# A transformer block on one core: the first expert item is chosen from twelve token tiles, and its first four product blocks stand between the last attention units

## The chip, the cores and the metric

The kernel runs on one core of a Trainium2 chip. The metric is the device time of one execution in microseconds (us). A core has five engines with queues of their own: TensorE (PE, with its weight loads PEld), VectorE (DVE), ScalarE (ACT), GpSimd (POOL) and the DMA queues, here nearly all issued from SyncE (SP). Each engine takes its instructions in the order in which they were recorded and waits on semaphores of the others.

## The reference

```python
# 1. windowed attention, 4 batches x 8 heads x 576 positions x 64
scores = where(0 <= i - j < 128, q @ k.T / 8 - slope[h] * |i - j|, -1e9)
x = softmax(scores) @ v                      # then [2304, 512], heads side by side
# 2. mixture of experts, one of 8 experts for each token
logits = x @ w_gate + modality_bias[modality_id]
e = argmax(logits);  gate = softmax(logits)[e]
x = gate * (relu(x @ w1[e]) @ w2[e])         # w1 512x1024, w2 1024x512
# 3. dense block
h = x @ w_in;  out = (h * cos(h)) @ w_out    # 512x2048, 2048x512
```

## The kernel before

Every fp32 product is made as three products of rounded parts (high by high, high by low, low by high), so each operand that comes from memory is split first: ScalarE casts the high part, VectorE subtracts it to get the low part. A split of a piece of weights (128 by 1024) is one CAST `s<-r` on ACT and one TENSOR_TENSOR `s<-r,s` on DVE.

**Attention.** There are 36 units: 18 tiles of 128 tokens, each in two halves of four heads. For a unit, `score(n)` makes the products q by k on PE, the masked minimum on DVE (`sx`) and the exponentials on ACT (`e`); `flip(n)` transposes the exponentials on PE, copies them on ACT (`pT`, `pa`) and masks them on POOL; `pv(n)` multiplies by v on PE and divides on DVE (`den`, then `xt` or `y`) into a tile X. The one accumulator bank O that `pv` writes must have been read by that division before the next `pv` may start. When both halves of a tile are there, it is stored to x_dram, and `xt_split` transposes it and splits it into xT.

**Routing.** For each pair of tiles, `logits(t)` gives three calls: the products with the gate weights (PE `bk<-xT,wg`, ACT `ls`), `choose` (two transposes of `ls` on PE, then eight short operations on DVE that end in `ohb`), and `ranks` (eight products of `ohb` and `cum` on PE, then DVE). `early()` picks the expert with most tokens so far, computes the row numbers of 256 of its tokens, gathers them from x_dram (an indirect DMA from POOL into xg, two halves) and loads that expert's first weights: this is item 0. In this kernel it looks at sixteen tiles (TE = T - 2). `late()` makes the full plan once all 18 tiles are ranked: `sums`, `slots` (ends in `oa<-oa,row` on DVE), `table` (18 products `oa` by `ob` on PE, then the row numbers `idx`), and `behind_slots` (ends in `regs<-ie`, the expert of each item, which SP reads before it can load that expert's weights).

**Items.** Nine items of 256 tokens follow. An item has eight up blocks (`up`: 12 products `xT,s` of 128x256) and eight down blocks (12 products `hh,s`), the downs three blocks behind the ups. `to_xT` transposes the two gathered halves and splits them (ACT CAST and DVE TENSOR_TENSOR `xT`).

**What sets the order.** In attention up to the fourth unit from the end PE and POOL are held to the written order; after that, the loop still calls score, flip and pv, and the calls in the list `after` (the logits of the last four tiles, `early()`, ...) are dealt out between them, while a list scheduler is free to order PE. In the items from block 12 to 67 the order is held again. Item 0's weights are split, and its rows transposed, only after the attention's pools are closed (the `split_w1(0, 0)`, `to_xT(0, 0)` lines ahead of the item loop).

Of the kernel before, what the change touches and what calls it, by code (L numbers as in the profile page):

```python
# [29 lines left out]
def kernel(  # L30
# [25 lines left out]
    UNITS = NE - 1  # L56
    NBLK = 2 * MIN_ITEMS + UNITS
    NL = MIN_ITEMS + UNITS
    TE = T - 2
# [160 lines left out]

    E = {}
# [41 lines left out]
    def early():  # L263
        eo = rt.tile([128, NE], F32, name="eo")
        w0 = rt.tile([128, TE], F32, name="w0")
        oa0 = rt.tile([128, TE, 2], F16, name="oa0")

        def first():
            m = rt.tile([128, 2], F32, name="em")
# [5 lines left out]
            V_.tensor_scalar(eo, rev, m[:, 1:2], None, op0=ALU.is_equal)  # L275
            fold(w0, oh[:, 0:TE], eo.unsqueeze(1).to_broadcast([128, TE, NE]), [128, TE, NE], rt)
            V_.tensor_tensor(w0, w0, row[:, 0:TE], op=ALU.mult)
            one_hot(oa0, 2, pf[:, 0, 0:TE], TE)
# [20 lines left out]
        return [first, second, order]  # L299
# [3 lines left out]
    def late():  # L303
# [116 lines left out]
        def rows_of():  # L420
# [4 lines left out]
            V_.tensor_tensor(dt, dt, rank, op=ALU.add)  # L425
            di = rt.tile([128, T], I32, name="di")
# [35 lines left out]
    def gather(i, u=None):  # L462
        for j in range(2 if u is None else 1):
# [13 lines left out]


# [23 lines left out]
    with ExitStack() as c:  # L502
# [261 lines left out]
        def pv(n):  # L764
# [11 lines left out]
            if hg == 0:  # L776
                X[t] = gp.tile([128, DM], F32, name="y") if t >= TE else xp.tile([128, DM], F32, name="xt")
# [3 lines left out]
            if hg == 1:  # L781
                with ExitStack() as w:
                    if t >= TE:
# [3 lines left out]
                if t < TE - 2:  # L787
                    later(p, 0, lambda: xt_split(t))
                else:
                    after.append(lambda: xt_split(t))  # L790
                if t % 2:
                    calls = logits(t - 1)
                    if t < TE - 2:
                        later(p, 1, calls[0])
                        later(p + 1, 0, calls[1])
                        later(p + 2, 1, calls[2])
                    else:
                        after.extend(calls)
                if t == TE - 1:
                    after.extend(early())  # L800

        def xt_split(t):
# [3 lines left out]
            for kk in range(KD):  # L806
                nc.tensor.transpose(pt[:, kk], X[t][:, 128 * kk:128 * kk + 128], ident)
            nc.scalar.copy(xT[:, 0, :, c0:c0 + 128], pt)
            nc.vector.tensor_tensor(xT[:, 1, :, c0:c0 + 128], pt, xT[:, 0, :, c0:c0 + 128].bitcast(F32),
                                    op=ALU.subtract)  # L810
# [49 lines left out]
        after, due = [], {}  # L860
# [55 lines left out]
        for n in range(N + 2):  # L916
# [4 lines left out]
            nc.tensor.on = n <= END + 1  # L921
# [5 lines left out]
            if n > END:  # L927
                calls([after.pop(0) for _ in after[:2]])
# [15 lines left out]
            if n > END:  # L944
                calls([after.pop(0) for _ in after[:2 if n < N + 1 else 1]])
        assert not due

    nc = tc.nc
    banks(S=2, T=2, P=2, O=1)
# [6 lines left out]
    W1, W2, HH, ACC = {}, {}, {}, {}  # L956
    NF = FF // 128
# [29 lines left out]
    def load_y(g, j, yT):  # L987
        yT = YT[g] = yT.rearrange("p a (k c) -> p a k c", k=KD)[:, :, :, 0:128 * groups[g][1]]
# [119 lines left out]
    with ExitStack() as c:  # L1108
# [3 lines left out]
        def split_w1(i, g):  # L1112
            s1 = W1[i, g] = s1s[(NF // 2 * i + g) % len(s1s)]
            r1 = R1.pop((i, g))
            nc.scalar.copy(s1[:, 0], r1)
            nc.vector.tensor_tensor(s1[:, 1], r1, s1[:, 0].bitcast(F32), op=ALU.subtract)

# [8 lines left out]
        def up(i, f):  # L1126
            g, j = divmod(f, 2)
            w, xT = W1[i, g], xTs[i % 2]
            if j == 0:
                HH[i, g] = bank("S", [128, 2, SLOTS])  # L1130
            ph = HH[i, g]
            for kk in range(KD):
                for a, b in ((0, 0), (0, 1), (1, 0)):
                    nc.tensor.matmul(ph[:, j], w[:, a, kk, 128 * j:128 * j + 128], xT[:, b, kk],
                                     start=kk == 0 and a == 0 and b == 0, stop=kk == KD - 1 and a == 1)
# [68 lines left out]
        split_w1(0, 0)  # L1204
        to_xT(0, 0)
        after.pop(0)()
        xt = to_xT(0, 1)
        after.pop(0)()
        split_w1(0, 1)
        after.pop(0)()  # L1210
        with tc.issue_after(xt[0].ins), tc.issue_after(MK["oh"].ins):
            splits(2, 1)
        for n in range(len(steps) + LAG):
# [67 lines left out]
            with ExitStack() as later:  # L1281
# [3 lines left out]
                if n < len(steps) and not InOrder.on:  # L1285
                    splits((n + 1) // 2 + 3, n // 2 + 1)
# [195 lines left out]
```

## Time and profile before

| | |
|---|---|
| median of 3 runs | 840.37 us (837.58 to 842.68) |
| profiled execution | 839.8 us, of which the span from first to last instruction is 838.1 us |
| busy share of the span | PE 95%, PEld 84%, DVE 73%, ACT 59%, POOL 24% |
| mean granted TensorE clock | 0.988 of full speed |

The span divides into attention with routing (0 to about 180 us), the expert items (about 180 to 420 us) and the dense block. The change touches the seam between the first two, about 153 to 226 us. A share of busy time says little there, since PE is nearly always busy on both sides of it; the rows of the seam itself are needed.

### The profile page before, as it was taken

The numbers are of one execution on the slowest core, as the hardware profiler recorded it, in microseconds if no ns is written. First come the engines' busy times: TensorE is split into PE (matmuls) and PEld (weight loads), VectorE is DVE, ScalarE is ACT, GpSimd is POOL, SyncE is SP. The second block draws the span as 40 slices with busy tenths as digits, with TensorE's granted clock in tenths as the row PEclk, the third lists the DMA queues.
The fourth block names the chain that finished last, engine by engine and source line by source line (L and its number), as shares of the span: only waits on it lengthen the run. The fifth ranks groups of instructions, "written<-read, shape, count | busy, mean of one in ns | idle before, by whom it ended". The sixth has DMA issues, their size and how long they took to land. (4 is left out here: it accounts for less than half of the span.)

```text
span 838.1 us, 14758 instructions
## 1 busy us (share of the span) xinstructions
PE 799.5 (95%) x5282; PEld 703.1 (84%) x5282; DVE 614.3 (73%) x1466; ACT 493.0 (59%) x912; POOL 200.6 (24%) x256
## 2 busy tenths in 40 slices
PE   8999999969899999999999999999999999999996
PEld 5889888958889999999878788787788888888995
DVE  4767786669899999995849999896665555555662
ACT  6866766543565776664647676754544555454562
POOL 4755574411022132330001221112122002100100
PEclk9999999979999999999999999999999999999999
DMA  9764530163888888869433231502212001100000
GB/s 164 166 152 108 139 90 33 40 206 117 268 272 266 283 277 274 280 206 334 159 116 91 79 125 54 174 25 79 85 43 71 1 1 40 36 1 1 26 26 25
DMA packets 125134, 103.40 MB, mean 123 GB/s; under 512 B 61725, under 2 KB 105027, under 8 KB 125059
## 3 DMA queue, kind: packets, MB, share of 16 engines
q1 hardware_dynamic: 121043, 92.48, 36.9%
q0 software_dynamic: 2960, 9.70, 3.3%
q8 instruction: 42, 0.69, 0.4%
q10 hardware_dynamic: 1056, 0.26, 0.2%
q14 instruction: 33, 0.27, 0.1%
HBM read 85.90 MB, written 16.52 MB: 122 GB/s over the span
## 5 line engine op out<-in xcount | busy, mean ns | idle before, releaser
L1096 PE MATMUL bk<-hh,s 128*128 128x256 f32 x864 | 117.5, 284 | 6.8 <-DVE y L1096 3.6
L1096 PE MATMUL bk<-xT,s 128*128 128x256 f32 x864 | 115.7, 283 | 1.7 <-DVE s L1096 1.1
L1096 PEld LDWEIGHTS bk<-hh,s 128*128 128x128 f32 x864 | 108.1, 189 | 8.8 <-DVE y L1096 4.4
L1096 POOL TENSOR_TENSOR lf<-lf,mag 128x512 f32<-128x512 f32 x32 | 47.4, 1482 | 282.1 <-DVE mag L1096 249.4
L1096 PEld LDWEIGHTS bk<-xT,s 128*128 128x128 f32 x864 | 108.2, 190 | 2.2 <-DVE s L1096 1.3
L1096 ACT CAST s<-r 128x1024 fp32r<-128x1024 f32 x72 | 75.3, 1051 | 55.1 <-DMA r<-in_moe_w_dram 38.3
L1096 PE MATMUL bk<-yT,wi_a 128*128 128x512 f32 (+1 forms) x480 | 104.4, 368 | 1.2 <-DVE yT L1096 0.8
L1096 PE MATMUL bk<-yT,wi_b 128*128 128x512 f32 (+1 forms) x480 | 105.0, 368 | 0.0
L1096 DVE TENSOR_TENSOR s<-r,s 128x1024 fp32r<-128x1024 f32 x72 | 94.2, 1310 | 13.9 <-ACT s L1096 13.3
L1096 ACT ACTIVATE r<-r 128x512 f32<-128x512 f32 (+1 forms) x80 | 47.2, 590 | 94.2 <-DVE r L1096 94.2
L1096 PEld LDWEIGHTS bk<-yT,wi_a 128*128 128x128 f32 x480 | 84.0, 188 | 17.2 <-DVE yT L1096 1.1
L1096 PEld LDWEIGHTS bk<-yT,wi_b 128*128 128x128 f32 x480 | 84.7, 188 | 15.7
L1096 DVE TENSOR_TENSOR r<-bk,r 128x512 f32<-128x512 f32 (+1 forms) x80 | 50.9, 637 | 62.4 <-ACT r L1096 61.7
L1096 PE MATMUL bk<-wo_b,gg 128*128 128x512 f32 x384 | 93.6, 391 | 2.4 <-DVE po L1096 1.1
L1096 PE MATMUL bk<-wo_a,gg 128*128 128x512 f32 x384 | 92.7, 390 | 0.4 <-DVE gg L1096 0.3
L1096 PEld LDWEIGHTS bk<-wo_b,gg 128*128 128x128 f32 x384 | 71.3, 188 | 19.6 <-issue 1.3
L1096 PEld LDWEIGHTS bk<-wo_a,gg 128*128 128x128 f32 x384 | 71.9, 188 | 16.1 <-DVE gg L1096 1.2
L1096 DVE TENSOR_TENSOR gg<-r,gg 128x512 fp32r<-128x512 f32 x64 | 46.2, 722 | 34.1 <-ACT gg L1096 34.1
L491 PE MATMUL bk<-vt,pT 128*128 128x65 f32 x544 | 65.9, 274 | 0.1
L491 PEld LDWEIGHTS bk<-vt,pT 128*128 128x128 f32 x544 | 64.1, 193 | 1.2 <-issue 1.0
L1096 ACT CAST gg<-r 128x512 fp32r<-128x512 f32 x64 | 39.7, 620 | 40.6 <-DVE r L1096 40.5
L1096 DVE SCALAR_TENSOR_TENSOR r<-ki,bk 128x512 f32<-128x512 int32 (+1 forms) x80 | 50.4, 630 | 16.5 <-ACT ki L1096 15.9
(283 smaller groups left out, 1275.9 us busy)
## 6 DMA issues: line engine op xcount, KB each, us to landing
r<-in_moe_w_dram SPq DMA_DIRECT2D x72, 512.0 KB
y_dram<-y SPq DMA_DIRECT2D x19, 256.0 KB
rqk<-in_q_dram SPq DMA_DIRECT2D x32, 128.0 KB
vt<-in_v_dram SPq DMA_DIRECT2D x32, 128.0 KB
x_dram<-xt SPq DMA_DIRECT2D x16, 256.0 KB
f64x<-in_moe_w_in_dram SPq DMA_DIRECT2D x8, 512.0 KB
raw<-in_moe_w_dram SPq DMA_DIRECT2D x8, 512.0 KB
yg<-y_dram SPq DMA_DIRECT2D x16, 256.0 KB
```

The source lines that it names most:

```text
L491: self.last = op(*args, **kwargs)
L1096: r = op(*args, **kwargs)
```

## The change

`early()` looks at the first twelve tiles rather than sixteen (TE = T - 6) and is called in seven parts, spread over the steps of units 30 to 33. Item 0's gather and its first weight loads therefore stand some units before the end of attention. If the chosen expert has fewer than 256 tokens among the twelve tiles, `lacks()` leaves the missing slots empty and shifts the plan (`short`); with the inputs used here it is zero. The loop stops two units early, and the rest of attention is written out by hand, with PE held to it: the scores of the last two units, `split_w1(0, 0)` and `split_w1(0, 1)` into a free slot of the attention's kT pool (`s1k`), `to_xT(0, ...)`, the last flips and pv, and `up_products(0, 0)` to `(0, 3)`. The item loop then skips the products of those four blocks. The PSUM banks are redealt (`banks(S=2, T=2, P=2, O=1)`) inside that list. The stores of the last two tiles stay behind item 0's first weight loads. The space for the plan grows by one unit (UNITS), which moves some buffers (xT0 from byte 199968 of a partition to 199744; yT0 starts at byte 82752, and the split weights start at multiples of 64 in both kernels), and the last group of the dense block reads its yT from 32 bytes further on (`off`).

```diff
-    UNITS = NE - 1
+    UNITS = NE
-    TE = T - 2
+    TE, TX = T - 6, T - 2
...
+        def lacks():
+            short = E["short"] = rt.tile([128, 1], F32, name="short")
+            V_.tensor_scalar(short, m[:, 0:1], -1.0, float(SLOTS), op0=ALU.mult, op1=ALU.add)
+            V_.tensor_scalar(short, short, 0.0, None, op0=ALU.max)
+            V_.scalar_tensor_tensor(cum[0:1], eo[0:1], short[0:1], cum[0:1], op0=ALU.mult, op1=ALU.add)
+            one_hot(oa0, 2, pf[:, 0, 0:TE], TE)
...
-            gather(0)
+        def rows0():
+            gather(0, half=0)
             load_w1(0, 0)
             load_w1(0, 1)
             MK["w"] = load_w2(0, 0)
+
+        def rows1():
+            gather(0, half=1)
...
+            V_.tensor_scalar(dr, dr, E["short"][0:1], None, op0=ALU.subtract)
...
+            V_.tensor_scalar(cond, dt, float(SLOTS), E["short"], op0=ALU.is_ge, op1=ALU.mult)
+            V_.tensor_tensor(dt, dt, cond, op=ALU.subtract)
...
+                    if t == TE - 1:
+                        for at, fn in zip((6, 7, 8, 10, 11, 12, 13), early()):
+                            later(p + at // 2, at % 2, fn)
...
-        for n in range(N + 2):
+        for n in range(N - 2):
...
+        kw = ktp.tile([128, 2, 2, 9 * 128], F32R, name="kT").rearrange("p a b c -> p (a b c)")
+        s1k = [kw[:, 2048 * g:2048 * (g + 1)].rearrange("p (a k c) -> p a k c", a=2, k=KD) for g in range(2)]
+        last14, last16 = logits(TX - 2), logits(T - 2)
+        nc.gpsimd.on = False
+        run(score(N - 2))
+        xt_split(TX - 1)
+        run(flip(N - 3))
+        pv(N - 4)
+        run(score(N - 1))
+        banks(S=2, T=2, P=2, O=1)
+        last14[0]()
+        with behind("dve", "act"):
+            split_w1(0, 0, s1k[0])
+        to_xT(0, 0)
+        to_xT(0, 1)
+        run(flip(N - 2))
+        last14[1]()
+        pv(N - 3)
+        run(flip(N - 1))
+        with behind("dve", "act"):
+            split_w1(0, 1, s1k[1])
+        up_products(0, 0)
+        last14[2]()
+        xt_split(T - 2)
+        pv(N - 2)
+        pv(N - 1)
+        up_products(0, 1)
+        xt_split(T - 1)
+        up_products(0, 2)
+        last16[0]()
+        up_products(0, 3)
+        nc.tensor.on = False
+        after = last16[1:]
...
+        off = 8 if w < 512 else 0
+        yT = YT[g] = yT.rearrange("p a (k c) -> p a k c", k=KD)[:, :, :, off:off + w]
...
-            w, xT = W1[i, g], xTs[i % 2]
-            if j == 0:
-                HH[i, g] = bank("S", [128, 2, SLOTS])
+            if i or f >= NF // 2:
+                up_products(i, f)
...
-        split_w1(0, 0)
-        to_xT(0, 0)
         after.pop(0)()
-        xt = to_xT(0, 1)
         after.pop(0)()
-        split_w1(0, 1)
-        after.pop(0)()
-        with tc.issue_after(xt[0].ins), tc.issue_after(MK["oh"].ins):
+        with behind("act", "dve"):
             splits(2, 1)
```

The first place is TensorE at the end of attention. Before (`vt,pT` is pv, `y` a last tile, `xg` the gathered rows of item 0, `s` its weights):

```order
L491 MATMUL bk<-vt_140,pT 128x65 x4
L491 MATMUL bk<-ident,y 128x128 x4
L1096 MATMUL bk<-xT_98,wg 16x256 x4
L1096 MATMUL bk<-ident,xg_99 128x128 x4
L1096 MATMUL bk<-xT_98,wg 16x256 x4
L1096 MATMUL bk<-ident,xg_100 128x128 x4
L1096 MATMUL bk<-ident,ls 128x16 x2
L1096 MATMUL bk<-xT_97,s_0_3423 128x256
```

TensorE at the same place in the changed kernel (`xT_97,kT` are item 0's products, `ohb,tri` the first of the ranks of tiles 14 and 15):

```order
L528 MATMUL bk<-ident,ls 128x16 x2
...
L528 MATMUL bk<-ident,e_3267 128x128 x4
L528 MATMUL bk<-xT_97,kT 128x256 x12
...
L528 MATMUL bk<-ohb,tri 128x8
...
L528 MATMUL bk<-ident,y 128x128 x4
L528 MATMUL bk<-vt_139,pT 128x65 x4
L528 MATMUL bk<-vt_140,pT 128x65 x4
L528 MATMUL bk<-xT_97,kT 128x256 x12
L528 MATMUL bk<-ident,y 128x128 x4
L528 MATMUL bk<-xT_97,kT 128x256 x12
L528 MATMUL bk<-xT_98,wg 16x256 x8
L528 MATMUL bk<-xT_97,kT 128x256 x12
```

The gathered rows moved ahead of the last flips, four blocks of item 0 stand between the last transposes and pv, and the ranks of tiles 14 and 15 stand behind the first of them.

The second place is VectorE between the logits of tiles 14 and 15 and the last pv, in the changed kernel (`kT<-r_3095` and `kT<-r_3097` are the low parts of item 0's first weights; `xT_97` its rows, `xT_98` tile 16):

```order
L869 TENSOR_TENSOR lg<-bk,biasm 128x16
L503 TENSOR_TENSOR kT<-r_3095,kT 128x1024
L496 TENSOR_TENSOR xT_97<-bk,xT_97 128x4x128 x2
...
L872 TENSOR_TENSOR lgs<-lg,lmx 128x16
L503 TENSOR_TENSOR kT<-r_3097,kT 128x1024
...
L876 TENSOR_TENSOR ohb<-rev,lm_3336 128x16
...
L811 TENSOR_SCALAR den<-bk 128x4
L218 TENSOR_TENSOR ob<-iota,pf 128x256
L842 TENSOR_TENSOR xT_98<-bk,xT_98 128x4x128
L812 RECIPROCAL den<-den 128x4
L815 TENSOR_TENSOR y<-bk,den 128x256
```

Before, these short operations of the choice stood among the `sx` operations of the last score:

```order
L838 TENSOR_REDUCE lmx<-lg 128x2
L730 ISA sx,nm<-bk,bias 128x128
...
L839 TENSOR_TENSOR lgs<-lg,lmx 128x16
...
L842 TENSOR_TENSOR oh<-rev,lm_3203 128x16
L843 TENSOR_TENSOR ohb<-rev,lm_3203 128x16
L775 RECIPROCAL den<-den 128x4
L778 TENSOR_TENSOR y<-bk,den 128x256
```

So two low parts of weights and two of rows moved into the choice of tiles 14 and 15.

The third place is VectorE ahead of the low part of item 1's first weights. Before, from the second half of item 1's rows on:

```order
L1096 TENSOR_TENSOR xT_98<-bk,xT_98 128x4x128
L413 RECIPROCAL gate<-gate 128x18
...
L425 TENSOR_TENSOR dt<-dt,rank 128x18
L1096 TENSOR_TENSOR s_1_3424<-r_3652,s_1_3424 128x1024
L427 CAST di<-dt 128x18
```

After:

```order
L1157 TENSOR_TENSOR xT_98<-bk,xT_98 128x4x128
L419 TENSOR_SCALAR dr<-dr,short 1x17
L429 TENSOR_REDUCE gate<-ex 128x18
L420 SCALAR_TENSOR_TENSOR regs<-blocks,dr 1x17
L430 TENSOR_SCALAR gate<-gate 128x18
...
L443 TENSOR_TENSOR dt<-dt,rank 128x18
L444 TENSOR_SCALAR cond<-dt,short 128x18
L445 TENSOR_TENSOR dt<-dt,cond 128x18
L447 CAST di<-dt 128x18
L1157 TENSOR_TENSOR s_1_3503<-r_3665,s_1_3503 128x1024
```

Seven more short operations stand between the rows and the weights: three are new, four stood elsewhere before.

## Rows read from the trace of the kernel before

**Rows 1.** The page: the span, and PEclk in 40 slices of 20.95 us
```profile
span 838.1 us, 14758 instructions
...
PEclk9999999979999999999999999999999999999999
```

**Rows 2.** Busy time by stage (PE, PEld, DVE, ACT, POOL; then PEclk, DMA share, GB/s)
```profile
176.00:184.00 8.00, 4.25 (x33) 2.79 (x34) 4.45 (x8) 2.67 (x3) 2.13 (x2) 0.56 0.99 321
190.00:200.00 10.00, 9.68 (x82) 9.48 (x81) 9.82 (x41) 3.98 (x6) 0.00 (x0) 1.00 0.35 109
```

**Rows 3.** Timeline of PE, 153 to 225 us (start, us, ..., [idle before <-releaser])
```profile
153.15 0.98 PE L491 MATMUL bk<-kT,qT 64*128 64x256 f32 x12
154.06 0.29 PE L491 MATMUL bk<-ident,ls 16*128 16x16 f32 x2
154.28 0.66 PE L491 MATMUL bk<-ident,e 128*128 128x128 f32 x4
154.78 1.90 PE L491 MATMUL bk<-vt,pT 128*128 128x65 f32 x16
156.51 0.61 PE L491 MATMUL bk<-ident,e 128*128 128x128 f32 x4
...
173.03 1.00 PE L491 MATMUL bk<-vt,pT 128*128 128x65 f32 x8
175.96 0.55 PE L491 MATMUL bk<-oa,ob 128*128 128x2 f16 x16 [1.92 <-DVE oa L279]
176.59 1.54 PE L491 MATMUL bk<-vt,pT 128*128 128x65 f32 x8
...
186.69 0.39 PE L1096 MATMUL bk<-ident,ls 16*128 16x16 f32 x2
...
213.97 2.87 PE L1096 MATMUL bk<-xT,s 128*128 128x256 f32 x22 [1.13 <-DVE s L1096]
...
224.61 0.50 PE L1096 MATMUL bk<-hh,s 128*128 128x256 f32 x2 [0.80 <-DVE hh L1096]
```

**Rows 4.** Granted clock in half microseconds (PE busy, PEclk, DMA share, GB/s)
```profile
177.00:177.50 0.50, 0.50 (x4) 0.52 1.08 377
187.50:188.00 0.50, 0.43 (x2) 1.00 1.07 346
252.00:252.50 0.50, 0.50 (x6) 0.62 1.06 375
255.50:256.00 0.50, 0.50 (x6) 0.97 0.99 334
```

**Rows 5.** Timeline of DVE: plan, then item 1's rows and first weights
```profile
190.15 0.16 DVE L214 TENSOR_TENSOR fold<-bk,oh 128x16 f32<-128x16 f32 x1
...
202.29 0.61 DVE L377 TENSOR_TENSOR oa<-oa,row 128x450 f16<-128x450 f16 x1
...
210.78 0.69 DVE L1096 TENSOR_TENSOR xT<-bk,xT 128x512 fp32r<-128x512 f32 x1 [0.65 <-ACT xT L1096]
...
212.70 1.22 DVE L1096 TENSOR_TENSOR s<-r,s 128x1024 fp32r<-128x1024 f32 x1
```

**Rows 6.** Timeline of ACT: the cast of item 1's first weights
```profile
210.82 1.05 ACT L1096 CAST s<-r 128x1024 fp32r<-128x1024 f32 x1
```

**Rows 7.** Groups of DVE instructions, 186 to 214 us (count | busy us, mean ns)
```profile
L1096 DVE SCALAR_TENSOR_TENSOR hh<-bk,hh 128x512 fp32r<-128x512 f32 x4 | 2.7, 684 | 0.1
```

**Rows 8.** The tile xg, 170 to 215 us: its gathers
```profile
DMA to landing us min/median/max: 3.5/6.7/7.4
```

**Rows 9.** Timeline of PE in two places with products of 256 columns
```profile
263.03 1.59 PE L1096 MATMUL bk<-xT,s 128*128 128x256 f32 x12
264.45 1.58 PE L1096 MATMUL bk<-hh,s 128*128 128x256 f32 x12
...
788.92 7.36 PE L1096 MATMUL bk<-yT,wi_a 128*128 128x256 f32 x60
796.11 1.55 PE L1096 MATMUL bk<-wo_a,yT 128*128 128x512 f32 x6
```

More of the change, by code (lines that the diff above doesn't have):

```diff
@@ L219, in one_hot @@
                          at.unsqueeze(2).to_broadcast([128, count, n]), op=ALU.is_equal)
+    NF = FF // 128
+    W1, HH = {}, {}
     E = {}
@@ L266, in early @@
         oa0 = rt.tile([128, TE, 2], F16, name="oa0")
+        m = rt.tile([128, 2], F32, name="em")
         def first():
-            m = rt.tile([128, 2], F32, name="em")
             rev, c = E["rev"], E["rp"][:, 2]
@@ L297, in order @@
             V_.tensor_tensor(M, key.unsqueeze(2).to_broadcast(shp), key.unsqueeze(1).to_broadcast(shp), op=ALU.is_gt)
-        return [first, second, order]
+        return [first, lacks, where, second, rows0, rows1, order]
     def late():
@@ L460, in late, with gather @@
         return [sums, slots, table, behind_slots], [starts, gates, rows_of, dense]
-    def gather(i, u=None):
-        for j in range(2 if u is None else 1):
+    def gather(i, u=None, half=None):
+        for j in range(2 if u is None else 1) if half is None else (half,):
             ap = idx0[:, j:j + 1] if i == 0 else idx[:, 2 * i + j:2 * i + j + 1] if u is None else \
@@ L476, in to_xT, with split_w1, up_products @@
         return ins, nc.vector.tensor_tensor(xT[:, 1, :, cs], pt, xT[:, 0, :, cs].bitcast(F32), op=ALU.subtract)
+    def split_w1(i, g, s1=None):
+        s1 = W1[i, g] = s1s[(NF // 2 * i + g) % len(s1s)] if s1 is None else s1
+        r1 = R1.pop((i, g))
+        nc.scalar.copy(s1[:, 0], r1)
+        nc.vector.tensor_tensor(s1[:, 1], r1, s1[:, 0].bitcast(F32), op=ALU.subtract)
+    def up_products(i, f):
+        g, j = divmod(f, 2)
+        w, xT = W1[i, g], xTs[i % 2]
+        if j == 0:
+            HH[i, g] = bank("S", [128, 2, SLOTS])
+        ph = HH[i, g]
+        for kk in range(KD):
+            for a, b in ((0, 0), (0, 1), (1, 0)):
+                nc.tensor.matmul(ph[:, j], w[:, a, kk, 128 * j:128 * j + 128], xT[:, b, kk],
+                                 start=kk == 0 and a == 0 and b == 0, stop=kk == KD - 1 and a == 1)
     class Turns:
@@ L776, in pv @@
             if hg == 0:
-                X[t] = gp.tile([128, DM], F32, name="y") if t >= TE else xp.tile([128, DM], F32, name="xt")
+                X[t] = gp.tile([128, DM], F32, name="y") if t >= TX else xp.tile([128, DM], F32, name="xt")
             nc.vector.tensor_tensor(
@@ L786, in pv @@
                 p = 2 * t + 2 + LP
-                if t < TE - 2:
+                if t < TX - 1:
                     later(p, 0, lambda: xt_split(t))
-                else:
-                    after.append(lambda: xt_split(t))
-                if t % 2:
+                if t % 2 and t < TX - 1:
                     calls = logits(t - 1)
[L793 to L800, printed above, removed]
+                    later(p, 1, calls[0])
+                    later(p + 1, 0, calls[1])
+                    later(p + 2, 1, calls[2])
+                    if t == TE - 1:
+                        for at, fn in zip((6, 7, 8, 10, 11, 12, 13), early()):
+                            later(p + at // 2, at % 2, fn)
         def xt_split(t):
@@ L807, in xt_split @@
                 nc.tensor.transpose(pt[:, kk], X[t][:, 128 * kk:128 * kk + 128], ident)
-            nc.scalar.copy(xT[:, 0, :, c0:c0 + 128], pt)
-            nc.vector.tensor_tensor(xT[:, 1, :, c0:c0 + 128], pt, xT[:, 0, :, c0:c0 + 128].bitcast(F32),
-                                    op=ALU.subtract)
+            MARK["act"] = nc.scalar.copy(xT[:, 0, :, c0:c0 + 128], pt)
+            MARK["dve"] = nc.vector.tensor_tensor(xT[:, 1, :, c0:c0 + 128], pt, xT[:, 0, :, c0:c0 + 128].bitcast(F32),
+                                                  op=ALU.subtract)
         def logits(t):
@@ L859 @@
         LF, LP = 2, 3
-        after, due = [], {}
+        due = {}
         def later(step, at, fn):
@@ L926 @@
             calls(due.pop((n, 0), []))
-            if n > END:
-                calls([after.pop(0) for _ in after[:2]])
             flips = [flip(m) for m in range(N) if turned[m] == n]
@@ L955 @@
     ytiles = [yt0.tile([128, 2, KD * 512], F32R, name="yT0")]
-    W1, W2, HH, ACC = {}, {}, {}, {}
-    NF = FF // 128
+    W2, ACC = {}, {}
     wp = pool(bc, "wp", 1, "right")
@@ L1110 @@
         cv = pool(cvs, "cv", 1, "right")
[L1112 to L1116, printed above, removed]
         def split_w2(i, g):
@@ L1127, in up @@
             g, j = divmod(f, 2)
-            w, xT = W1[i, g], xTs[i % 2]
-            if j == 0:
-                HH[i, g] = bank("S", [128, 2, SLOTS])
+            if i or f >= NF // 2:
+                up_products(i, f)
             ph = HH[i, g]
[L1132 to L1135, printed above, removed]
             if j:
@@ L1285 @@
                 if n < len(steps) and not InOrder.on:
-                    splits((n + 1) // 2 + 3, n // 2 + 1)
+                    with behind(*("act", "dve")[:2 if n < 2 else 0]):
+                        splits((n + 1) // 2 + 3, n // 2 + 1)
                 if n < len(steps) and not InOrder.on:
```

10 lines of the change are left out of this document (3 added, 7 removed).

## The prediction

> **What bounds the kernel now.** I read the page first. The granted clock is full in every slice of the span but one, the ninth, from 168 to 189 us [rows 1], and that slice is the seam that the change rewrites. The table by stages shows why: from 176 to 184 us TensorE is busy for 4.25 of 8 us at a mean clock of 0.56, while from 190 to 200 us VectorE is busy for 9.82 of 10 [rows 2]. So two engines bound the seam in turn: TensorE first stands still, then VectorE is full. The timeline of PE gives the places. It waits 1.92 us for VectorE's choice of item 0's rows; soon after, the two last pv are followed by the stores, the gather and its data, and the transposes for the last logits come only at 186.69 [rows 3]. The clock falls to half 3 us after that wait began, at about 177, and comes back between 187.0 and 187.5 [rows 4]. A last bound lies behind it: item 1's up blocks run freely from 213.97, held by the low part of their weights on VectorE [rows 3].
>
> What the change could win at most is the idle time and the slow clock between the last score and 213.97. I lay the changed order out with the durations of the rows and see where it waits.
>
> **TensorE up to the logits of tiles 14 and 15.** I start at 153.15, where both programs stand at the same score [rows 3]. A score takes 0.91, four transposes 0.50, a pv 1.73, two transposes of logits 0.22 (each from one start to the next). Up to and with those logits the new order holds four scores, 3.64; seven sets of four transposes (flips and tiles), 3.5; four pv, 6.92; eight gate products at two thirds of a block's 1.42 [rows 9], 0.95; two sets of transposes of item 0's rows, 1.0; twelve products for those rows instead of sixteen (0.63 for sixteen), 0.45; eight products of ranks by the same row, 0.3; the logits' own 0.2. That is 17.0, so 170.1. Item 0's gather hides: its row numbers come from about 154.5, POOL can issue after the masks of that step, near 159, and even the slowest landing of 7.4 us [rows 8] makes 166.6, before the rows are transposed at about 168.6. The three weight loads beside it are as early. If that cover were gone, each us past 168.6 would go straight into the sum.
>
> **The first new wait.** From 170.1 TensorE goes on with a pv and a flip, to 172.3. VectorE meanwhile does one short operation (about 0.17), a low part of weights, 1.22, and two of rows, 0.69 each [rows 5]: 172.9, which holds the first block of item 0 for 0.6 us. That block ends at 174.3, and next in TensorE's order stand the ranks of tiles 14 and 15. They need `ohb`, and ahead of `ohb` stands the second low part of weights, whose cast on ScalarE stands behind the copy of the flip that ended at 172.3: copy 0.6, cast 1.05 [rows 6], 174.0; low part 1.22, 175.2; the half tile's division and four short operations, 1.1: 176.3. TensorE waits 2.0 us, with the transposes, pv and three blocks behind it in its queue.
>
> **The second.** Ranks 0.3, transposes 0.5, a pv of half size 0.87 [rows 3]: 178.0. The next pv needs the one bank O back, and VectorE's order between is `den`, `ob`, the low part of tile 16, the reciprocal and `y`: 0.2, 0.4, 0.7, 0.2, 0.4, so 179.9, a wait of 1.9.
>
> **The clock.** After a wait of 1.92 it fell to half 3 us from the wait's start [rows 3, 4]; another fall, at 252.2, ended at about 255.5 with TensorE busy all the while, 3.3 us. The new waits are of that size, so I take a fall at 177.3 and a return 3.3 us after 179.9: some 4 us of work at half rate, 2.0 us lost. The Trainium skill (TensorE: Matmul & The Clock Gate, section "Why this matters for your kernels") lists only idle gaps longer than either of these waits as what brings the clock down. By that page these 2.0 us would not be lost; the trace, where 1.92 was enough, does not agree with it.
>
> **The plan.** From 179.9: pv 0.87, three blocks 4.26, transposes 0.5, gate products 0.95, logits 0.2, so 186.7 and with the clock 188.7. In the trace this place is 186.69 with its row of 0.39 [rows 3]: the four blocks done ahead have eaten the gain here. VectorE then has a short operation, a low part of weights, another short one, a low part of hh (0.68 [rows 7]) and six short ones: 3.3, so 192.0; on TensorE 33 products stand before the ranks, 3.9, so 192.6 and 192.9 with them. From the ranks to the end of `oa` it was 12.75 before [rows 5]; three low parts of weights and two of hh (3.66 and 1.37) no longer stand in it, so 7.7 to 7.9. `oa` ends at 200.8 instead of 202.9. This is the change's gain on the chain that counts, 2.1 us, and TensorE has its 69 products up to the table done at about the same time.
>
> **Item 1.** From the end of `oa` to item 1's free run took 11.07 us (202.90 to 213.97): table, row numbers, gather, rows, then the weights' low part. Before, 1.2 us of short operations stood between the rows' low part and the weights'; now seven more do, 1.2 us at 0.17. The weights' cast ended 0.8 ahead of its low part [rows 5, 6], which covers the low part of hh that now stands before the expert's number. So 12.3, that is 213.1: gain 0.85. Behind the table TensorE has only 18 products left until then, 2.1 us, and will wait some 7 us in all, so the clock falls here too, as it did not before: 1.6 us by the fall at 252.2, of which VectorE's old wait of 0.80 at 224.61 [rows 3] hides half. Net 0.8 lost. It could be nothing, if VectorE alone sets the pace there, or 3.3, if the clock needs twice as long.
>
> **Small terms.** Four products fewer: 0.1. The moved buffer: 60 products that read yT took 7.19 us, 119.8 ns each, where twelve that read xT took 1.42, 118.3 [rows 9]. yT0 starts at a multiple of 64 bytes as the weights do, xT0 did not and now does; if that is the cause, 864 products pay 1.5 ns, 1.3 us, and the last group's 192, now moved off, win 0.3. No row shows it to be the cause, so the bounds are 0 and 1.3, and I take 0.65 in the middle. Work in `lacks`, `first` and `where` lies in VectorE's gaps of the units before.
>
> **The sum**, against the profiled execution's 839.8: minus 0.85, plus 0.8, plus 0.65, minus 0.3, minus 0.1, so plus 0.2: 840.0. The median of the runs shown is 840.4, 0.6 above that execution. About 0.5%, 4.2 us, is what can be told from no change.
>
> **Rivals.** The waits aren't there (faster). If the second weights' low part and the last tiles come as soon as TensorE wants them, 3.9 us of waits and the 2.0 of the clock go from the chain: item 1 runs at 207.2, total 834.1. For it speaks that TensorE before also lost some 1.2 us between 153 and 173 to gaps too short for a row, and whatever makes it later makes the waits shorter; against it, that both waits follow from the order alone and their operations' lengths are in rows. Chance 0.20.
>
> The clock stays up through both waits: `oa` at 198.8, item 1 at 211.1, total 838.0. This is what the page's rule would give, with the later, longer wait still dropping it. The fall after 1.92 us speaks against it. Chance 0.13, a third of which I let reach past 0.5%.
>
> The clock stays down (slower). Before, it was at half for 10.3 us at this seam. If the two waits and what is between them keep it down as late as 193 us, through the last logits and the first downs, 10 us more at half rate put 4.9 on the chain: 844.9. It decides from about 9 us more at half rate. Against it: TensorE is busy nearly throughout from 179.9, where before it stood still for most of the slow stretch. Chance 0.12.
>
> The change doesn't do what it says: item 0's rows or weights come after 168.6 and everything waits for them; at 5 us late, 845. Chance 0.03.
>
> **Numbers.** The forecast, no change that can be told, has 0.52, with its own range of 837 to 843. With the rivals: faster by over 0.5% 0.25, within 0.60, slower 0.15. The range for 8 in 10 reaches toward both sides, 834 to 844.5.
>
> **What would show it.** Right: PE idle of about 2 us before the ranks of tiles 14 and 15, and of about 1.9 before the last pv; half clock from about 177 to 183 and again around item 1's first block; the last logits near 188.7, `oa` near 200.8, item 1 free near 213.1. Wrong: waits under 1 us at these places, or a clock that stays full; or item 1 running before 209.

## The result, and the profile after

The changed kernel is slower: 852.33 us in the median of 4 runs (845.70 to 856.39), beside 841.52 for the kernel before (837.58 to 843.05). The ratio is 1.0121 (95% interval 1.0080 to 1.0162). My 840.0 was wrong, and 852.33 lies outside my range of 834 to 844.5. In the comparisons below, ratios and mean clocks, though not medians, leave out three runs that were unusually long: two of e8's eleven (855.66 and 855.71 us; with them its mean clock is 0.981 instead of 0.983) and one of the kernel before (851.53).

The page of the changed kernel, where the rows answer to [rows 1]. The slices are 21.3 us long.

```profile
span 850.8 us, 14757 instructions
...
PEclk9999999789799999999999999999999999999999
```

The span is 12.7 us longer than before, and the reader sees it in one line: before, one slice of the clock stood under full, now three do, the 8th, 9th and 11th (149 to 191 and 213 to 234 us). The loss is at the seam, and TensorE's clock is in it.

The timeline of PE at the seam, to be read beside [rows 3]. The bracket holds the idle time before a row and what ended it.

```profile
153.47 0.98 PE L528 MATMUL bk<-kT,qT 64*128 64x256 f32 x12
154.38 0.45 PE L528 MATMUL bk<-oa,ob 128*128 128x2 f16 x12
156.20 0.29 PE L528 MATMUL bk<-ident,ls 16*128 16x16 f32 x2 [1.37 <-DVE idx L298]
156.42 0.66 PE L528 MATMUL bk<-ident,e 128*128 128x128 f32 x4
156.92 2.93 PE L528 MATMUL bk<-vt,pT 128*128 128x65 f32 x16
...
167.09 3.01 PE L528 MATMUL bk<-vt,pT 128*128 128x65 f32 x16 [1.02 <-DVE xt L815]
...
179.15 0.29 PE L528 MATMUL bk<-ident,ls 16*128 16x16 f32 x2
...
185.49 0.18 PE L528 MATMUL bk<-ohb,tri 128*128 128x8 bf16 x1 [1.66 <-DVE ohb L876]
...
189.01 1.94 PE L528 MATMUL bk<-vt,pT 128*128 128x65 f32 x8 [1.82 <-DVE y L815]
...
198.46 0.30 PE L1157 MATMUL bk<-ident,ls 16*128 16x16 f32 x2
...
222.37 0.79 PE L1157 MATMUL bk<-xT,s 128*128 128x256 f32 x2 [3.92 <-ACT s L1157]
223.63 5.06 PE L1157 MATMUL bk<-xT,s 128*128 128x256 f32 x22 [0.46 <-DVE s L1157]
```

Two waits stand here that my sum doesn't have: 1.37 us at 156.20 and 1.02 us at 167.09. The first pv behind each is slow as well: 2.93 and 3.01 us, where one took 1.90 before [rows 3].

The first wait's releaser is `idx`, and VectorE's timeline says why it is late.

```profile
155.15 0.28 DVE L767 CUSTOM_DVE_ANT_0 sx<-bk,bias 128x128 f32<-128x128 f32 x1
...
155.78 0.29 DVE L767 CUSTOM_DVE_ANT_0 sx<-bk,bias 128x128 f32<-128x128 f32 x1
...
155.99 0.15 DVE L298 TENSOR_SCALAR idx<-bk 128x2 int32<-128x2 f32 x1
```

`second()` writes the twelve index products into bank `L`, which has one buffer. VectorE reads them (`idx`) only behind the four `sx` of the score that TensorE made just before. The next thing in TensorE's order, the transposes of the logits of tiles 12 and 13 (`choose`), wants bank `L` too. So they wait, and with them everything behind.

The granted clock, by stretches (us, then busy time of PE, PEld, DVE, ACT and POOL, then PEclk, DMA share, GB/s).

```profile
154.00:157.50 3.50, 2.13 (x32) 1.88 (x29) 2.50 (x16) 1.59 (x5) 1.02 (x2) 1.00 0.81 283
157.70:164.40 6.70, 6.70 (x38) 6.14 (x38) 3.07 (x17) 1.35 (x4) 3.72 (x6) 0.50 0.10 40
164.50:167.80 3.30, 2.28 (x22) 2.17 (x20) 0.94 (x4) 1.56 (x5) 2.02 (x3) 1.00 0.60 159
168.00:174.60 6.60, 6.60 (x44) 6.36 (x43) 3.40 (x21) 2.05 (x6) 0.00 (x0) 0.50 0.10 41
174.80:188.20 13.40, 10.38 (x97) 9.29 (x96) 8.73 (x37) 7.06 (x14) 1.22 (x2) 1.00 0.43 126
188.40:195.10 6.70, 6.09 (x28) 6.12 (x29) 2.32 (x6) 1.19 (x3) 0.00 (x0) 0.50 0.34 102
219.10:229.30 10.20, 6.46 (x28) 6.17 (x29) 9.89 (x27) 6.28 (x9) 0.58 (x1) 0.50 0.85 292
```

Each new wait was followed by about 6.8 us at the lower level, 1.2 GHz (the rows bracket it with 6.7 and 6.6), with PE busy in all of it: about 3.4 us lost each time, more than the waits themselves. A third such stretch begins inside the wait before the last pv (187.2 to 189.0), which I had forecast, and a fourth lies at item 1.

### The profile page after: what moved, and what is told of

Same layout as the page of the kernel before. It is cut to its first block, busy times and chain, and to the rows that moved or that the text cites. A ratio compares the mean times of both kernels' runs of the same rounds, so it can differ in the third digit from the quotient of the medians.

```text
span 850.8 us, 14757 instructions
## 1 busy us (share of the span) xinstructions
PE 807.8 (95%) x5278; PEld 713.0 (84%) x5278; DVE 615.1 (72%) x1472; ACT 492.2 (58%) x912; POOL 199.0 (23%) x256
## 5 line engine op out<-in xcount | busy, mean ns | idle before, releaser
L1157 PE MATMUL bk<-xT,s 128*128 128x256 f32 x816 | 111.9, 287 | 4.4 <-ACT s L1157 3.9
L1157 PEld LDWEIGHTS bk<-xT,s 128*128 128x128 f32 x816 | 104.8, 195 | 4.9 <-ACT s L1157 4.2
L1157 ACT CAST s<-r 128x1024 fp32r<-128x1024 f32 x70 | 73.0, 1049 | 55.6 <-DMA r<-in_moe_w_dram 40.1
L528 PE MATMUL bk<-vt,pT 128*128 128x65 f32 x544 | 69.1, 282 | 2.8 <-DVE y L815 1.8
L528 PEld LDWEIGHTS bk<-vt,pT 128*128 128x128 f32 x544 | 67.2, 201 | 4.1 <-issue 2.9
L770 ACT ACTIVATE e<-sx,nm 128x128 f32<-128x128 f32 (+1 forms) x144 | 51.5, 421 | 22.4 <-DVE nm L767 22.0
```

Source lines behind the costliest of these rows:

```text
L528: self.last = op(*args, **kwargs)
L770: MARK["act"] = nc.scalar.activation(e[:, h, :wv], x[:, :wv], AF.Exp, bias=nm[:, h:h + 1], scale=-1.0)
L1157: r = op(*args, **kwargs)
```

## The experiments

The theory (A): the two waits that I missed, and the half rate behind them, make most of the loss. Its rivals: the written order costs it wherever those rows stand (B); the moved buffers do, in the steady stretches (C). A fourth came up on the way (D): time saved before the last logits comes back as waits of item 1, whose products were moved forward. Each kernel was timed beside the kernel before on the same chip; the experiments ran in three sets, and the changed kernel's ratio is to the 841.52 above.

| kernel | median us | ratio to before (95%) | mean granted clock of the timed runs |
|---|---|---|---|
| before, in the three sets | 841.6, 842.4, 842.6 | 1 | 0.985, 0.985, 0.984 |
| changed | 852.33 | 1.0121 (1.0080 to 1.0162) | 0.976 |
| e4, first wait filled | 851.76 | 1.0112 (1.0068 to 1.0157) | 0.980 |
| e8, second wait gone | 846.92 | 1.0061 (1.0025 to 1.0097) | 0.983 |
| e1, first wait gone | 844.84 | 1.0043 (1.0018 to 1.0069) | 0.981 |
| e2, both gone | 842.75 | 1.0012 (0.9986 to 1.0039) | 0.983 |
| e3, early choice alone | 841.16 | 1.0008 (0.9985 to 1.0030) | 0.985 |
| e5, e2 and the forecast waits covered | 839.05 | 0.9977 (0.9948 to 1.0007) | 0.987 |
| e9, e5 and item 1's waits filled | 839.15 | 0.9962 (0.9938 to 0.9986) | 0.993 |
| e10, e5 and the address of before | 841.65 | 0.9975 (0.9947 to 1.0002) | 0.986 |
| e11, e9 and e10 | 840.40 | 0.9977 (0.9956 to 0.9999) | 0.992 |
| e6, early choice, index later | 838.93 | 0.9969 (0.9944 to 0.9994) | 0.986 |
| e12, e6 and the address of before | 836.99 | 0.9941 (0.9912 to 0.9970) | 0.986 |

**e1: the first wait.** The index products go half a step back, behind `choose`, and the gathers and first weight loads go half a step back with them.

```diff
-                        for at, fn in zip((6, 7, 8, 10, 11, 12, 13), early()):
+                        for at, fn in zip((6, 7, 8, 11, 12, 13, 13), early()):
```

> The changed kernel with one entry of the table moved: the products that make the first item's index go from ahead of the logits' transposes of tiles 12 and 13 to half a step behind them, the loads and the order behind them move along. Theory A, the wait that I had missed (1.37 us at 156.20, for the one bank of the logits) and the fall of the clock at 157.65 behind it cost the most: that wait and that fall are gone, 1.4 + 3.4 = 4.8 us less than the changed kernel's 852.3, so about 847.5; the fall at 167.9 with the 1.02 us wait stays. Theory B, the written order costs it wherever the index products stand: within 1 us of 852. Theory C, the moved buffers' addresses cost it in the steady stretches: within 1 us of 852, and the clock's fall at 157.65 gone all the same.

Measured: 844.84, and the half rate from 157.7 on is gone. In the timeline of e1's PE the logits' transposes come at once, the index products stand behind them, and the wait for bank O is left.

```profile
154.52 0.29 PE L528 MATMUL bk<-ident,ls 16*128 16x16 f32 x2
...
157.47 0.44 PE L528 MATMUL bk<-oa,ob 128*128 128x2 f16 x12
...
162.59 3.04 PE L528 MATMUL bk<-vt,pT 128*128 128x65 f32 x16 [1.02 <-DVE xt L815]
```

The clock of e1 between the two:

```profile
156.50:160.00 3.50, 3.50 (x46) 3.28 (x45) 2.76 (x16) 1.92 (x6) 2.37 (x5) 1.00 0.33 125
160.00:163.00 3.00, 1.98 (x19) 1.87 (x17) 1.97 (x10) 1.71 (x6) 2.80 (x4) 1.00 0.29 90
```

One entry of a table took away 1.21 - 0.43 = 0.78 per cent, 6.6 us, where theory A had 4.8. B and C had expected at most 1 us of gain. Both fall as the main cause.

**e8: the second wait.** In the written order pv(31) stands right behind pv(30), and both want the one bank O. The scheduler of the kernel before had put the next unit's scores between them.

```diff
+            if n == N - 3:
+                run(score(N - 2))
             for m in sums[1:]:
                 pv(m)
...
-        run(score(N - 2))
```

> The changed kernel with the scores of the last unit but one between the two sums of units 30 and 31, and the index products where the change put them. Theory A: the 1.37 us wait and the fall at 157.65 stay, the 1.02 us wait and the fall at 167.89 go: 4.4 us under the changed kernel's 852.3, about 848. If the second fall comes from the first wait and not from the second: only 1.0 us less, 851, with the half rate at 168 still there.

Measured: 846.92, ratio 1.0061, as expected for the time (0.60 per cent, 5.1 us less). But the trace gave a surprise. Here is e8's first wait in the timeline of PE.

```profile
159.35 0.29 PE L528 MATMUL bk<-ident,ls 16*128 16x16 f32 x2 [1.37 <-DVE idx L298]
159.57 0.66 PE L528 MATMUL bk<-ident,e 128*128 128x128 f32 x4
160.06 1.90 PE L528 MATMUL bk<-vt,pT 128*128 128x65 f32 x16
```

And this is the clock of the six us around it:

```profile
157.00:163.00 6.00, 4.63 (x58) 4.21 (x58) 3.73 (x22) 2.43 (x7) 2.45 (x4) 1.00 0.54 178
```

It is the same wait, between the same instructions, and no half rate follows. So a single profile doesn't tell what a wait of this size costs through the clock. The table's last column, a mean over timed runs, points the way of theory A: 0.976 for the changed kernel, 0.981 and 0.983 with one of the waits gone.

**e2: both.** e1 and e8 together.

> The kernel of e1 with the scores of the last unit but one put between the two attention sums of units 30 and 31, where the kernel before had them, so that the sum of unit 31 doesn't wait 1.02 us for the one bank that the sum of unit 30 still holds. Theory A: the wait and the fall of the clock at 167.89 are gone as well, 1.0 + 3.4 us less than e1, about 843; the logits of tiles 14 and 15 then end at about 170 instead of 179.2. Theory B (the order of the tail itself): the time stays at 851 to 852, since the 2.0 us wait before the ranks and the 1.8 us wait before the last sum are still there. Theory C: 851 to 852.

Measured: 842.75, as theory A said, and no longer to be told from the kernel before. The two savings add up to a little more alone (0.78 and 0.60) than together (1.09), a difference within the intervals. In e2's timeline pv(31) doesn't wait; the transposes behind it wait 0.54 us for the same row of VectorE. The logits of tiles 14 and 15 stand at 171.22 instead of 179.15.

```profile
165.43 0.44 PE L528 MATMUL bk<-ident,xt 128*128 128x128 f32 x2 [0.54 <-DVE xt L815]
...
171.22 0.29 PE L528 MATMUL bk<-ident,ls 16*128 16x16 f32 x2
...
177.56 0.18 PE L528 MATMUL bk<-ohb,tri 128*128 128x8 bf16 x1 [1.65 <-DVE ohb L876]
...
182.10 1.94 PE L528 MATMUL bk<-vt,pT 128*128 128x65 f32 x8 [1.82 <-DVE y L815]
...
191.57 0.29 PE L1158 MATMUL bk<-ident,ls 16*128 16x16 f32 x2
```

**e4: is it the wait or the clock?** Seven products that nothing uses stand in the first wait; the second stays.

```diff
+                    if t == TE + 1:
+                        later(p + 1, 0, lambda: warm(*[512] * 7))
                     later(p + 1, 0, calls[1])
```

> The changed kernel with seven dummy products of 512 columns, of no use to the result, between the index products and the logits' transposes of tiles 12 and 13, so that the wait for the bank is still there and TensorE works through it. Theory A with the clock as the larger part: the half-rate stretch from 157.65 is gone, 3.4 us less, about 848.5 to 849; the second fall at 167.9 stays. If the wait alone counts, and the clock falls for another reason: 852 and the stretch still there. Theories B and C: within 1 us of 852.

Measured: 851.76, no gain, where theory A had 848.5 to 849. Here are e4's added products and its second wait in the timeline of PE.

```profile
154.74 2.97 PE L528 MATMUL bk<-still 128*128 128x512 bf16 x7
...
165.37 2.78 PE L528 MATMUL bk<-vt,pT 128*128 128x65 f32 x16 [1.02 <-DVE xt L815]
```

The clock of e4 in two stretches:

```profile
154.00:166.00 12.00, 10.65 (x97) 8.09 (x93) 7.17 (x36) 4.72 (x12) 6.33 (x10) 1.00 0.38 131
166.50:180.00 13.50, 13.50 (x80) 12.43 (x80) 5.11 (x32) 5.06 (x13) 1.25 (x3) 0.50 0.09 36
```

The half rate behind the first wait is gone, as expected. But the products took 2.97 us, 1.4 longer than the wait (the transposes stand at 157.64 instead of 156.20), and behind the second wait the clock stayed at half for some 13.5 us instead of 6.7. What was won at one place was paid at the other. As a test of wait against clock it is inconclusive, and how the loss divides between the waits and the half rate rests on the mean clocks, not on an experiment that parts them.

**e3: one part alone.** The early choice by the change's own table, with the loop, the `after` list and the item loop's first blocks as in the kernel before.

```diff
-        for n in range(N - 2):
+        for n in range(N + 2):
...
+            nc.tensor.on = n <= END + 1
...
-        run(score(N - 2))
-        xt_split(TX - 1)
...
+        split_w1(0, 0)
+        to_xT(0, 0)
+        after.pop(0)()
+        xt = to_xT(0, 1)
```

> The changed kernel's early choice from 12 tiles alone, by its own table, with the tail of attention left to the scheduler as in the kernel before, and the first item's products after it. Theory A: the bank's wait of 1.4 us and its fall of the clock stay, the 1.02 us wait goes, the index no longer lies behind the last logits: before's 841 plus 4.8, less 1 to 2 for the index products and gathers, plus 1.0 for the buffers' addresses if they lie as in the changed kernel: 844 to 847. Theory B: without the written order no loss, 839 to 841. Theory C: 841 to 842.

Measured: 841.16, ratio 1.0008, below theory A's 844 to 847. e3 still has the first wait in its timeline of PE:

```profile
156.26 0.29 PE L528 MATMUL bk<-ident,ls 16*128 16x16 f32 x2 [1.37 <-DVE idx L298]
```

and again no half rate behind it:

```profile
157.00:164.00 7.00, 7.00 (x72) 6.48 (x70) 5.24 (x24) 3.44 (x8) 4.64 (x7) 1.00 0.19 57
```

The early choice by itself costs nothing that can be told. What e3 lacks is the written order, and with it the second wait, whose place the scheduler fills with the next scores, as it did before. It also lacks the forecast wait before the ranks and the four blocks moved ahead, so e3 alone doesn't divide the loss; e1, e8 and e2 do.

**e5: the forecast waits.** e2 with the tail's last pieces dealt again: a block of item 0 between the last two pv, the ranks behind it, another block before the transposes (the new argument names the parts of a block that are done).

```diff
         up_products(0, 0)
-        last14[2]()
         xt_split(T - 2)
         pv(N - 2)
-        pv(N - 1)
         up_products(0, 1)
+        last14[2]()
+        pv(N - 1)
+        up_products(0, 2)
         xt_split(T - 1)
-        up_products(0, 2)
+        up_products(0, 3, (0, 1))
         last16[0]()
-        up_products(0, 3)
+        up_products(0, 3, (2, 3))
```

> The kernel of e2 with the tail's last pieces in another order: the second quarter of the first item's products between the last two attention sums, the ranks of tiles 14 and 15 behind it, the third quarter between the last sum and its transposes, the last quarter in two halves around the last logits. In e2 TensorE waits 1.65 us before those ranks and 1.82 us before the last sum, and its half-rate stretch there is 10.2 us long (5.1 us lost). Theory A, waits in front of TensorE and the half rate behind them set the time: the last logits stand near 184 to 187 instead of 191.6, the free run starts as much earlier, and the time is 5 to 7 us under e2, 836 to 838. Theory D, which e3 suggests (it has no product moved forward and is no slower than e2): what the products moved forward cover in the tail is missing at the second item's waits, so time saved before the last logits comes back as longer waits behind the plan: the time stays within 1.5 us of e2, and the waits between 205 and 217 of e2 (6.8 us) grow by what is saved before.

Measured: 839.05, over theory A's 836 to 838 and below what theory D allows (841.25 or more). By the medians it is 3.7 us under e2, by the ratios 0.35 per cent, 2.9 us, with intervals that overlap. The two profiled runs alone lie 6.4 apart (838.78 and 845.14), but e2's was one of its longer ones. Here is e5's end of attention and item 1's free run in the timeline of PE.

```profile
177.11 0.44 PE L528 MATMUL bk<-ident,y 128*128 128x128 f32 x2 [1.05 <-DVE y L815]
...
185.72 0.29 PE L1159 MATMUL bk<-ident,ls 16*128 16x16 f32 x2
...
211.51 5.06 PE L1159 MATMUL bk<-xT,s 128*128 128x256 f32 x22 [1.47 <-DVE s L1159]
```

The clock around that run (the half rate runs from 203.7 to 217.3, not from 209 on, as e9's expectation below has it):

```profile
208.00:222.00 14.00, 11.29 (x82) 10.95 (x83) 12.66 (x32) 8.58 (x11) 0.00 (x0) 0.67 0.71 234
```

Both forecast waits are gone and one of 1.05 us is new. The last logits stand 5.85 us before e2's, and item 1's free run 5.0 us before (211.51 against 216.53). Item 1's four waits hold 6.8 us in both (2.24, 0.42, 2.70 and 1.47 here; 1.68, 0.96, 3.64 and 0.53 in e2), so theory D's growth didn't come. What is left of D: these waits are there at all. They hold 7.0 us in the changed kernel, 2.9 in the kernel before (0.89, 0.86 and 1.13) and 2.4 in e3, which has no block moved ahead; and in e5 half rate begins inside the first of them, where the kernel before has none until 252.

**e9: item 1's waits.** 36 products that nothing uses, around the index table and item 1's transposes, so that products of use are left for the waits (`still_on` issues so many products into one bank S, behind the instruction named).

```diff
                     elif f == 7:
+                        still_on(16, MK["regs"])
                         to_xT(1, 0)
-                        to_xT(1, 1)
+                        still_on(20, to_xT(1, 1)[0])
```

> The kernel of e5 with 36 products of the first item's input that nothing uses, put into the stretch around the index table and the second item's transposes, so that products of use are left for the second item's waits. In e5 TensorE waits 2.24, 0.42, 2.70 and 1.47 us there, and from 209 on runs 13.7 us at half rate. If the half rate behind those waits costs (theory A): the 4.3 us of added products lie in the waits, the half-rate stretch is gone or under 7 us, and the time is 2 to 5 us under e5's 839, so 834 to 837. If the chain of plan, weights' loads and splits sets the end whatever TensorE does in between (theory D): within 1 us of e5. If the added products stand on the chain: up to 4 us slower, 843.

Measured: 839.15, over theory A's 834 to 837 and within 1 us of e5, as theory D said; by the ratios, 0.9962 where e5 has 0.9977, it could be either, since the intervals overlap: unclear. In e9's profiled run the 22 products take 2.90 us instead of 5.06,

```profile
210.74 2.90 PE L1159 MATMUL bk<-xT,s 128*128 128x256 f32 x22 [1.32 <-DVE s L1159]
```

and the half rate is gone:

```profile
208.00:222.00 14.00, 11.31 (x103) 10.52 (x102) 13.15 (x31) 10.04 (x13) 0.00 (x0) 1.00 0.76 241
```

Its span of 833.6 is the shortest of all, but its timed runs go up to 843.82. Their mean clock is 0.993, where e5 has 0.987, and the median is the same: the clock came up and the time didn't follow. Where it went stays open.

**e6 and e12: without the written order.** e6 is e3 with e1's table; e12 adds the address of before.

> The early choice alone (e3) with the index products half a step behind the logits' transposes of tiles 12 and 13, as e1 has it. In e3 the wait of 1.37 us stands at 156.26, but the clock stayed up behind it. Theory A: only that wait goes, 1.4 us under e3, 839 to 840, and no half-rate stretch more or less before 180. If the clock's fall hangs on the wait alone, e3's profile was the exception and its timed runs hold the fall: 3 to 5 us under e3, 836 to 838.

> The early choice without the written order, the index products behind the logits' transposes (e6), and the address of before. e6 came to 838.9 (0.997 of before); the address gives 1.0: 838. If it ties with e11, the written order is worth nothing beyond what the early choice gives.

Measured: 838.93 and 836.99. By the ratios e6 is 0.39 per cent, 3.3 us, under e3, where theory A had 1.4, but the two intervals overlap. As theory A said, no half-rate stretch more or less lies ahead of the last pv in e6 than in e3; in both it begins at the wait of 1.82 us there or right behind it (the mean clock from 150 to 178 is 1.00 in e3, and 0.97 in e6, where that wait stands 1.4 us earlier). e12 is the fastest of all, 0.59 per cent under the kernel before (0.30 to 0.88), and so beats it and the changed kernel. Against e5 and e9 to e11 the intervals overlap: the written order, mended, is worth nothing that can be told beyond the early choice.

**e7, e10 and e11: the address.** e7 is the kernel before with the item inputs at a multiple of 64 bytes; e10 and e11 put e5 and e9 back to 32 behind one.

```diff
+    rt.tile([128, 8], F32, name="gap1")
     xgs = [rt.tile([128, DM], F32, name=f"xg{j}") for j in range(2)]
...
     s2s = [wp.tile([128, 2, 2, DM], F32R, name=f"s2_{j}") for j in range(2)]
+    wp.tile([128, 8], F32, name="gap2")
```

> The kernel before, with 32 bytes put in so that the first item's input tiles begin at a multiple of 64 bytes, as in the changed kernel, and not 32 bytes behind one; nothing else moves against a multiple of 64. If the address costs, the products of these tiles take about 119.8 to 120 ns of each other instead of 118.3, and 816 of them 1.0 to 1.3 us; the time alone can't show that. If not, the products keep before's pace, and the changed kernel's slower pace has another cause.

> The kernel of e5 with the item inputs 32 bytes behind a multiple of 64 again, as in the kernel before. From e7, where the move the other way took the products from 118.3 to 119.3 ns, and the changed kernel's 119.7: the products of these tiles back at 118.3 ns, 0.9 to 1.1 us under e5, so about 838.

> e9 and e10 together. By theory A 833 to 836, about 0.8 per cent under the kernel before; by theory D 838.

e7 was run once (842.55 us), so only its products count. Measured by the product: two groups of e7's timeline, to be read beside [rows 9] from one start to the next.

```profile
263.36 1.60 PE L1098 MATMUL bk<-xT,s 128*128 128x256 f32 x12
264.80 1.58 PE L1098 MATMUL bk<-hh,s 128*128 128x256 f32 x12
```

Twelve products that read xT now take 1.44 us instead of 1.42. The mean from one product's start to the next, over some 500 such pairs between 270 and 780 us, is 119.3 ns in e7 (119.8 to 120 expected) and 119.7 in the changed kernel, 118.3 in the kernel before, and 116.8 in e10 (118.3 expected). So the place of the buffer does change the pace: 816 products pay 1.1 us in the changed kernel. By the time of e10 (0.9975 against 0.9977) and e11 (0.9977 against 0.9962) nothing can be told; with 841.65 and 840.40 they missed their 838 and 833 to 836.

## Why the prediction was wrong, by its own steps

**"TensorE up to the logits of tiles 14 and 15" is the step that failed.** I added up what TensorE does from 153.15 and came to 170.1, as if nothing in that stretch waited. I looked for new waits only behind it. The row stands at 179.15, 9.05 late. The two waits give 2.39, and two stretches of 6.8 us at half rate with PE busy throughout give 6.8, which with the 0.3 by which the start itself is later is 9.5, the 9.05 to half a us. I had named the index products only as a number of instructions, not as the holder of a bank that the next row needs, and two pv in a row only as twice 1.73. e2 changes these two places and what moves with them. It brings the row to 171.22 and the time to 1.0012 of before; the rest of the sum (840.0, 0.9995 of the median) lies within that interval. The means close as well: half rate can have cost e2 14.3 us, 6.5 less than the changed kernel, and e2's waits up to this row are 1.85 shorter; that is 8.4, and its mean time is 8.5 less (843.2 against 851.7, four runs of the changed kernel). It doesn't prove the rest of my sum: in e2's profiled run the steps from this row to item 1's free run took 45.3 us where I had 43.0.

**"The first new wait" and "The second" were right:** 0.6 before the first block, 2.0 before the ranks and 1.9 before the last pv forecast; 0.35, 1.66 and 1.82 measured. e2, where all before them had moved 8 us, has them unchanged (0.36, 1.65, 1.82), so they follow from the order alone, as the argument said.

**"The clock" was right in kind and too small.** I had one fall at 177.3 and 2.0 us lost. In e2, where no half rate stands ahead of these waits, it lasts 10.2 us there (178.0 to 188.3), and from the logits of tiles 14 and 15 to the last logits it takes 20.35 us where I had 18.6. The rival that the clock stays down is the nearest to what happened in the changed kernel (four stretches, 6.8, 6.8, 6.8 and 10.2 us between 157 and 230 and one of 3.4 at 413, where the kernel before has 10.2 and, at 252, 3.4), but it was to come from the waits that I knew. Over all timed runs half rate can have cost the changed kernel 20.9 us (1 less the mean clock, 0.0245, of the mean 851.7) and the kernel before 12.5 (0.0149 of 841.6): 8.4 of the 10.1 us between them. This is a bound, since half rate costs nothing where TensorE waits; e9 shows how loose it can be. The Trainium skill (TensorE: Matmul & The Clock Gate, section "Why this matters for your kernels") names only idle gaps longer than these waits of attention as what brings the clock down. The changed kernel's trace doesn't agree, with 1.37 and 1.02; e3's and e8's, where 1.37 us had no consequence, do.

**"The plan" and "Item 1":** from the last logits to the end of `oa` 13.2 us (211.67 less 198.46) where I had 12.1, and from there to item 1's free run 12.0 where I had 12.3. The gain on VectorE's chain is real: before it was 16.2 [rows 3, 5]. That item 1 took what I had forecast is partly luck. I had the cast of its first weights done 0.8 us ahead of their low part; in the changed kernel the cast itself waits 1.97 us for the weights to land, and ends just when VectorE's added short operations are done.

```profile
221.28 1.04 ACT L1157 CAST s<-r 128x1024 fp32r<-128x1024 f32 x1 [1.97 <-DMA r<-in_moe_w_dram]
...
222.35 1.22 DVE L1157 TENSOR_TENSOR s<-r,s 128x1024 fp32r<-128x1024 f32 x1
```

The waits there hold 7.0 us, as I had them (some 7), but the half rate with them lasts 10.2 us (219.0 to 229.2): the 22 products of the free run took 5.06 where they took 2.87 before, 2.2 lost where I had 0.8.

**"Small terms":** 816 products pay 1.1 us, of which I took 0.65 as the middle of 0 to 1.3. The last group won more than forecast, 0.6 for its 192 products where I had 0.3: 60 of them start at 802.13 and the next row at 809.13, 116.7 ns each instead of 119.8 [rows 9].

```profile
802.13 7.16 PE L1157 MATMUL bk<-yT,wi_a 128*128 128x256 f32 x60
809.13 1.55 PE L1157 MATMUL bk<-wo_a,yT 128*128 128x512 f32 x6
```

The steps from 179.15 on, taken together, are 1.5 us over my sum, and 2 more come behind 223.63, about what the slow 22 products lost. The missed stretch is 9 of the 12.5.

## What to carry to other kernels

When an engine is held to a written order, go through that order row by row and ask of each row which buffer it writes, who reads that buffer last, and what stands ahead of the reader on its own engine; a sum of durations finds no wait. A single-buffered bank that two neighbouring rows share is the place to look at first: here one entry of a table was worth 0.8 per cent. Work that is moved forward into waits is missing at the next ones (here 7.0 us of waits at item 1 instead of 2.9), so look at what is left for those before counting the gain; the early choice did as well without the written order as with it repaired.

## What the runs showed of the hardware that I had not expected

- The same wait of 1.37 us was followed by half rate in one profiled execution and not in two others, of which e3 has the same products in the same order from 120 us up to it. A wait of 1.43 or 1.44 us near 109 stands in the trace of every kernel here, and only in e8 does half rate follow it (111.0 to 114.4). Neither the wait's length nor the rows around it decide it alone. The Trainium skill (TensorE: Matmul & The Clock Gate, section "Part 1: The HAM clock gate (the "warmup" mystery)") says, of the products at a kernel's start, that the number of slow ones varies from run to run of one kernel; here the mean clock of the changed kernel's four runs goes from 0.968 to 0.981. What a wait costs through the clock is a mean over runs, and it differs by kernel: with both waits gone (e2) 0.983 against 0.976, but with the first gone from e3 (e6) 0.986 against 0.985.
- Products of one shape run at different paces by where their input begins. With the item inputs at a multiple of 64 bytes they start every 119.3 to 119.7 ns, on the mean, in all ten kernels that have them there; with the inputs 32 bytes behind one it is 118.3 (before) and 116.8 ns (e10 to e12). What parts the last two isn't shown: no run moves the weights or anything else alone.
- The seven products of 512 columns in e4 took 2.97 us at the full clock. They go into one bank, and in the trace each takes 0.38 us and waits on a semaphore that the one before it raises, so that they start 0.43 us apart, while products of 256 columns in one sum start every 0.12 us. Work put into a wait must be measured before it is called free.
